# An attention and GLU kernel whose instruction order is planned in Python: other latencies in the planner

## The chip, the cores and the metric

The kernel runs on one core of a Trainium2 chip. The core has a matrix engine (PE, with its weight loads shown apart as PEld), a vector engine (DVE), a scalar engine (ACT), GpSimd (POOL), and a queue for transfers (SP). Each engine takes its instructions in the order in which the program issues them; between engines, semaphores hold an instruction until what it reads is there. The metric is the device time of one execution in microseconds (us); the median of several is given.

## The reference

The input x has 2048 rows of 640 numbers in bf16. There are 32 heads of 20 columns.

```python
x = A_x
h = x + _A_ref(_layernorm(x, axis=-1), A_wqkv, A_wo)
h2 = h + _B_ref(_layernorm(h, axis=-1), B_w_gate, B_w_up, B_w_down)

# _A_ref: q, k, v = heads of x @ wqkv
scores = einsum("bhqd,bhkd->bhqk", q, k) * (20 ** -0.5)
p = softmax(scores, axis=-1)
o = einsum("bhqk,bhkd->bhqd", p, v)        # then o @ wo

# _B_ref: (x @ w_gate) * (x @ w_up), 1728 wide, then @ w_down
```

## The kernel before

**Tiles and stages.** The 2048 queries are cut into five chunks (three of 512, two of 256), the heads into eight groups of four. Scores are made transposed: a tile has 128 keys on the partitions and 512 query columns of one head (or twice 256 for two key tiles). There are 2048 such tiles. Four heads of a group lie on four 32-row strips of PE, so four score matmuls (line 992, mode "R") run side by side. The exponential of a tile is made in one of two ways. ACT takes three tiles at once from the PSUM set SA into a buffer EA, or two from the set SB into a buffer EB (line 1067). DVE takes one tile from one of the banks D0 and D1, with an approximation of four bit-shifted copies: a first pass from PSUM (line 1092), two adds on DVE and one on POOL (lines 1102 and 1100). The buffers are 5 EA, 4 EB and 28 Y. The exponentials are multiplied with V (line 1143, mode "C": four heads on four 32-column strips, adding up in the bank ACC); a tile of ACT needs one such matmul, a tile of DVE four. VX carries a column of ones, so ACC also gets the softmax's sums. When a head group is done, `close_group` copies ACC, sends the sums through DRAM to get reciprocals spread over the partitions, and POOL multiplies.

**Background jobs.** Projections for q, k and v, the output projection and the GLU are jobs of matmuls (line 1316 in strips during attention, line 1293 in whole-array form, mode "D", before and after it). During attention a job takes one of the two D banks; its result is copied out by DVE. Each job has a target, a place in the stream of score tiles by which it should have run.

**The order.** Nothing in the program is ordered by hand. While the kernel is built, Python runs a small event simulation: `now` is the planned time, each engine has a queue of ready instructions (`ready`, `coming`) sorted by a key, and whatever can start at the planned time is issued at once. The costs are formulas (`c_psum(512)` is 0.607 us, `c_fast(512)` 0.208, `c_act(1536)` 1.38, `c_act(1024)` 0.953, a 512-column matmul 0.216), and `LAT`, 0.12 us, lies between the end of any instruction and the start of whatever reads it or uses its buffer again. The planned times are not in the program; what remains is the order on each engine, the choice of which tiles go to DVE, and the choice of buffers.

**What decides around the change.**
- `try_start` takes the ready instruction with the lowest key: DVE's copies of closed groups have -2, evacuations 0, the first pass 1, the adds 2. `finish` tells the readers when they may start.
- `pe_turn` is called when PE is nearly done with what it has (0.03 us before its end, `pe_rest`). It first asks `to_refill`: if a set is free, `refill` issues a score round for it, together with a tile for DVE if a D bank may be had (`d_banks`: one tile on DVE at a time while a background job is ready, else two). If only one set is free, no D bank is, and ACT has more than `THR` = 0.7 us left, the refill waits. Otherwise PE makes up to `ROUNDS` = 4 rounds in columns (`c_round`), each some 0.22 us long, taking exponentials and background matmuls, and stops after the first if `urgent` says that a refill is possible or if a set comes free soon.
- A change between modes R and C costs the planner `SWITCH` = 0.105 us.
- `refill` sets the mark on which ACT's exponential waits, `fill_d` that of DVE's first pass, `emit_piece` the release of the buffer that a matmul of line 1143 has read, `close_group` the mark for ACC's copy, `job_done` the mark for a job's evacuation. Each is the planned end of a matmul plus `LAT`.

Of the kernel before, what the change touches and what calls it, by code (L numbers as in the profile page):

```python
# [14 lines left out]
ACT = mybir.ActivationFunctionType  # L15
# [42 lines left out]


LAT = 0.12  # L60
DMA_LAT = 1.5
SWITCH = 0.105

# [80 lines left out]
def kernel(  # L144
# [89 lines left out]
            heapq.heappush(coming[e], (op.avail, seq[0], op))  # L234
        tick(op.avail)

    def finish(op, t):
        op.done = t
        for u in op.users:
            u.left -= 1  # L240
            u.avail = max(u.avail, t)
            if u.left == 0:
                if isinstance(u, Op):
                    enqueue(u)
                else:
                    release_later(u.avail, u.cb)
        op.users = []
        tick(t)
# [31 lines left out]
    def try_start(e):  # L280
        t = now[0]
        if free[e] > t + 1e-9:
            return False
        c = coming[e]
        while c and c[0][0] <= t + 1e-9:
            _, s_, op = heapq.heappop(c)
            heapq.heappush(ready[e], (op.key, s_, op))
        held = []
        got = None
        while ready[e]:  # L290
            item = heapq.heappop(ready[e])
            op = item[2]
            if op.done is not None:
                continue
            if op.gate is not None and not op.gate():
                held.append(item)
                continue
            other = "POOL" if e == "DVE" else "DVE"
            if op.lock and e in lockt and lockt[other] > t + 1e-9:
                held.append(item)  # L300
                tick(lockt[other])
                continue
            got = op
            break
        for h_ in held:
            heapq.heappush(ready[e], h_)
        if got is None:
            return False
        end = t + (got.dur[e] if isinstance(got.dur, dict) else got.dur)
        free[e] = end  # L310
        if got.lock and e in lockt:
            lockt[e] = end
        if got.hook is not None:
            got.hook(t, end, e)
        got.fn(e)
        finish(got, end + got.lat)
        tick(end)
        return True

# [36 lines left out]
    with tc.manual_schedule():  # L356
# [595 lines left out]
        acs_n = [0]  # L952
        acs_use = [None, None]
        bc_use = [None]
        act_pend = [0]
        dve_units = [0]

        for ci in range(len(CHUNKS)):
# [57 lines left out]
        def refill(name, dbanks):  # L1016

            st = sets[name]
            st["state"] = "full"
            st["free_at"] = 1e9  # L1020
            used = set()
            ditems = []
            for i in dbanks:
                it = take_for_dve(used)
                if it is not None:
                    used.add(it[2])
                    ditems.append((i, it))
            items = []
            for i in range(st["n"]):
                it = take_next(used)  # L1030
                if it is not None:
                    used.add(it[2])
                    items.append(it)
            n = len(items)
            pairs = [(banks[name][i], items[i]) for i in range(n)] + [(banks["D"][i], it) for i, it in ditems]
            ends = rows_into(pairs)
            for q, (i, it) in enumerate(ditems):
                fill_d(i, it, ends[n + q])
            if not n:
                st["state"] = "free"  # L1040
                return
            end = max(ends[:n])
            src = (SA if name == "SA" else SBk)
            eslot = {}

            def hook(t, en, e):
                eslot["i"] = st["efree"].pop(0)
                left = [0]

                def rel():  # L1050
                    left[0] -= 1
                    if left[0] == 0:
                        st["efree"].append(eslot["i"])
                        tick(now[0])
                for i, it in enumerate(items):
                    left[0] += len(it[3])
                for i, it in enumerate(items):
                    queue_pieces(it, 3, [st["e"][eslot["i"]][:, i * 512:(i + 1) * 512]], en + LAT, rel)

                def fr():  # L1060
                    st["state"] = "free"
                    act_pend[0] -= 1
                release_later(en + LAT, fr)
                st["free_at"] = en + LAT

            def fn(e):
                nc.scalar.activation(st["e"][eslot["i"]][:, 0:n * 512], src[:, 0:n * 512], ACT.Exp, scale=SCALE)  # L1067
            z = Mark()
            z.done = end + LAT
            act_pend[0] += 1  # L1070
            add("ACT", c_act(512 * n), fn, (1,), [z], hook=hook, gate=lambda: bool(st["efree"]))

        def fill_d(i, it, end):
            bank = banks["D"][i]
            bank_use["D"][i] = "exp"
            z = Mark()
            z.done = end + LAT
            ys = [None] * 4
            dve_units[0] += 1

            def take(q):
                ys[q] = y_free.pop(0)
                y_owed[0] -= 1

            def hook(t, en, e):
                y_owed[0] += 4
                take(0)

                def fr():
                    bank_use["D"][i] = None  # L1090
                release_later(en + LAT, fr)
            p_ = add("DVE", c_psum(512), lambda e: nc.vector.tensor_scalar(  # L1092
                YT[ys[0]][:, :], bank, scalar1=EXP_A, scalar2=EXP_B, op0=ALU.mult, op1=ALU.add),
                (1,), [z], hook=hook, gate=lambda: len(y_free) - y_owed[0] >= 4)

            def s_op(dst, src_, d, eng, deps):
                def fn(e):
                    o, i_ = YT[ys[dst]][:, :], YT[ys[src_]][:, :]
                    if e == "POOL":
                        nc.gpsimd.tensor_scalar(o, i_, scalar1=float(d), scalar2=1.0, op0=ALU.add, op1=ALU.mult)  # L1100
                    else:
                        nc.vector.tensor_scalar(o, i_, scalar1=float(d), scalar2=None, op0=ALU.add)  # L1102
                return add(eng, {"DVE": c_fast(512), "POOL": c_pool(512)}, fn, (2,), deps, lock=True, lat=LAT,
                           hook=lambda t, en, e: take(dst))
            s1 = s_op(1, 0, SH[1], "DVE", [p_])
            s2 = s_op(2, 0, SH[2], "DVE", [p_])
            s3 = s_op(3, 2, SH[3] - SH[2], "POOL", [s2])
            left = [len(it[3])] * 4
            left[0] += 2
            left[2] += 1  # L1110

            def rel(q):
                left[q] -= 1
                if left[q] == 0:
                    y_free.append(ys[q])
                    tick(now[0])

            for o, q in ((s1, 0), (s2, 0), (s3, 2)):
                after([o], lambda q=q: rel(q))
            for q, o in enumerate((p_, s1, s2, s3)):  # L1120
                after([o], lambda q=q: queue_pieces(it, q, [YT[ys[q]][:, :].bitcast(BF16)], now[0], lambda: rel(q)))
# [11 lines left out]
        def emit_piece(j):  # L1133
# [8 lines left out]
            _, end = pe_issue("C", j, 0.216 * cw / 512)  # L1142
            nc.tensor.matmul(ACC[32 * j:32 * j + 32, 0:cw], lhsT=VX[:, kt, h * VS:h * VS + 32], rhs=ap,  # L1143
                             start=(n == 0), stop=last, tile_position=(0, 32 * j), skip_group_check=True)
            release_later(end + LAT, rel)
            if last:
                acc_state["left"] -= 1
                if acc_state["left"] == 0:
# [8 lines left out]
        def close_group(ci, g, end):  # L1157
            q0, cw = CHUNKS[ci]
            z = Mark()
            z.done = end + LAT  # L1160
            k = ngrp[0] % 2
            d = ngrp[0] % NDS
            ngrp[0] += 1
# [95 lines left out]
        def job_done(jb):  # L1259
            cur_job[0] = None  # L1260
            z = Mark()
            z.done = jb.end + LAT
            op = jb.evac(banks[jb.bank[0]][jb.bank[1]], z)
            bk = jb.bank

# [126 lines left out]
        def pe_turn():  # L1392
# [3 lines left out]
            if spos[0] >= len(stream):  # L1396
                attn["over"] = True
            else:
                r = to_refill()
                if r is not None:  # L1400
                    attn["started"] = True
                    refill(*r)
                    return pe_rest()
            n = 0
            over = attn["over"]
            while n < (1 if over else ROUNDS):
                if n and (urgent() or min(s_["free_at"] for s_ in sets.values()) < pe["end"] - 0.1):
                    break
                c = counts()
                if over and c is not None and sum(c) and c_round(c, False, False):  # L1410
# [7 lines left out]
                if not c_round(c, late and not short(), hold):  # L1418
                    break
                n += 1  # L1420
            return pe_rest() if n else False

        ROUNDS = 4
        WLO, WHI = 20, 50
# [27 lines left out]
        def to_refill():  # L1452
# [3 lines left out]
            if not names:  # L1456
                return None
            db = d_banks()
            if len(names) == 1 and not db and free["ACT"] - now[0] > THR and attn["started"]:
                tick(free["ACT"] - THR)  # L1460
                return None
            return names[0], db

        def urgent():
            return to_refill() is not None
# [73 lines left out]
```

The softmax here doesn't subtract the row's maximum and nothing guards it: scores larger than these inputs give would overflow.

## Time and profile before

| | |
|---|---|
| Median of 13 runs | 871.2 us (863.65 to 874.93) |
| Profiled execution | 873.31 us, of it 871.5 us span, mean granted clock 0.976 |
| PE, busy share of the span | 93% |
| DVE | 85% |
| ACT | 87% |
| POOL | 40% |
| First and last exponential on ACT start | 19.7 and 800.1 us |
| Exponentials on ACT: EA, EB | 319 and 315 |
| Tiles on DVE | 467 |
| Mean granted clock from 250 to 275 us, the lowest stage in attention | 0.84 |

In the lines of groups, "x319" is a count, then come busy time in all and the mean of one in ns, then the idle time of the engine just before these instructions and what ended most of it. In the lines of waits, the numbers are the time in all, the count and the longest. Matmul ends are modelled, so the starts of matmuls are the firm numbers. ACT and DVE instructions that follow each other overlap somewhat in the records: the durations add up to more than the time from start to start.

### The profile page before, as it was taken

The page shows a single profiled execution, that of the slowest core. Times are in us where ns is not written, and L with a number is a line of the kernel's source. Part 1 is how long each engine was busy: PE and PEld are TensorE (multiplying, and loading weights), DVE is VectorE, ACT ScalarE, POOL GpSimd, SP SyncE. Part 2 cuts the span into 40 slices and gives each one's busy share as a digit, 9 for nine tenths or more (in the row PEclk, how much of TensorE's full clock was granted, in tenths as well). Part 3 has the DMA queues.
Part 4 walks back from the last instruction along what each step waited for, and adds up shares of the span by engine and source line. Part 5 has one row for each costly group of instructions (what it writes and reads, how often), then busy time and mean ns, then how long its engine had stood idle before and what let it go on. Part 6 is the DMA issues. An engine that isn't in the chain of part 4 may idle for free.

```text
span 871.5 us, 34285 instructions
## 1 busy us (share of the span) xinstructions
PE 813.9 (93%) x14491; PEld 390.5 (45%) x14491; DVE 736.8 (85%) x2002; ACT 757.4 (87%) x711; POOL 352.4 (40%) x520
## 2 busy tenths in 40 slices
PE   4998999999999999999998999999899999999978
PEld 2432433433323444443233444444355555554856
DVE  6787999888889989998899999988999898896333
ACT  5788999999978999999998999999999999996211
POOL 1033444444443545444455445444545444443000
PEclk9999999999968999999899999999999999999989
DMA  8454221222135301111101002010111111003000
GB/s 271 65 161 127 95 73 39 90 81 75 51 99 129 99 23 46 33 45 31 33 24 32 22 22 53 21 44 27 34 35 41 41 32 35 21 16 52 26 16 16
DMA packets 70537, 49.64 MB, mean 57 GB/s; under 512 B 33712, under 2 KB 66448, under 8 KB 70384
## 3 DMA queue, kind: packets, MB, share of 16 engines
q1 hardware_dynamic: 70384, 47.46, 20.4%
q8 instruction: 113, 1.85, 0.9%
q14 instruction: 40, 0.33, 0.1%
HBM read 30.88 MB, written 10.32 MB: 47 GB/s over the span
## 4 chain that ended last, share of the span: by engine, by line
PE 63%; DVE 18%; ACT 9%; DMA 6%; issue 3%; SPq 0%; POOL 0%; DVEq 0%; ACTq 0%
PE D L1316 21%; PE ACC L1143 17%; PE SA L992 7%; PE D L1293 7%; DVE Y L1092 6%; DVE Y L1102 6%; PE SB L992 5%; ACT EA L1067 5%; PE D L992 5%; ACT EB L1067 4%; DMA dn<-dscr 2%; DMA dscr<-acs 1%; DVE acs L1172 1%; DMA qscr<-HH 1%; DMA R<-in_A_x_dram 1%
## 5 line engine op out<-in xcount | busy, mean ns | idle before, releaser
L1067 ACT ACTIVATE EA<-SA 128x1536 bf16<-128x1536 f32 x319 | 462.3, 1449 | 25.9 <-PE SA L992 17.3
L1100 POOL TENSOR_SCALAR Y<-Y 128x512 uint16<-128x512 uint16 x467 | 304.2, 651 | 415.1 <-DVE Y L1102 270.9
L1092 DVE TENSOR_SCALAR Y<-D 128x512 uint16<-128x512 f32 x467 | 317.9, 683 | 55.5 <-PE SB L992 18.9
L1067 ACT ACTIVATE EB<-SB 128x1024 bf16<-128x1024 f32 x315 | 324.7, 1031 | 19.7 <-PE SB L992 17.1
L1143 PE MATMUL ACC<-Y,VX 128*32 128x512 bf16 (+1 forms) x2356 | 269.0, 344 | 4.9 <-DVE acs L1172 3.5
L1102 DVE TENSOR_SCALAR Y<-Y 128x512 uint16<-128x512 uint16 x934 | 254.4, 318 | 3.1
L1143 PE MATMUL ACC<-EA,VX 128*32 128x512 bf16 (+1 forms) x1186 | 217.7, 346 | 1.2 <-ACT EA L1067 1.1
L992 PE MATMUL D<-QT,KTt 20*128 20x512 bf16 (+1 forms) x589 | 180.1, 343 | 11.7 <-DVE Y L1092 7.6
L992 PEld LDWEIGHTS <-KTt 20*128 20x128 bf16 x2560 | 72.5, 91 | 220.6 <-issue 210.8
L1143 PE MATMUL ACC<-EB,VX 128*32 128x512 bf16 (+1 forms) x785 | 170.8, 346 | 0.3 <-ACT EB L1067 0.3
L1316 PEld LDWEIGHTS <-R 128*32 128x32 bf16 x5370 | 125.0, 96 | 91.0 <-issue 71.4
L1143 PEld LDWEIGHTS <-VX 128*32 128x32 bf16 x4327 | 120.0, 97 | 99.5 <-issue 77.0
L992 PE MATMUL SA<-QT,KTt 20*128 20x512 bf16 (+1 forms) x1186 | 131.6, 345 | 9.3 <-ACT EA L1067 7.8
L1316 PE MATMUL D<-L,R 128*32 128x256 bf16 x3240 | 130.9, 276 | 1.8 <-DVE HH L826 1.4
L992 PE MATMUL SB<-QT,KTt 20*128 20x512 bf16 (+1 forms) x785 | 126.5, 344 | 2.7 <-ACT EB L1067 2.3
L1316 PE MATMUL D<-R 128*32 128x160 bf16 (+1 forms) x2130 | 106.3, 301 | 3.4 <-DVE VX L325 1.1
L826 DVE TENSOR_TENSOR HH<-D,gs 128x256 bf16<-128x256 f32 x112 | 46.8, 418 | 23.2 <-ACT gs L323 22.5
L1201 POOL TENSOR_TENSOR os<-acs,bc 128x512 bf16<-128x512 f32 (+1 forms) x40 | 43.4, 1085 | 48.5 <-DMA bc<-rscr 20.4
L1316 PE MATMUL D<-R,HH 128*32 128x320 bf16 x1136 | 55.3, 301 | 1.9 <-DVE HH L826 1.4
L323 ACT CAST gs<-D 128x256 bf16<-128x256 f32 (+1 forms) x28 | 10.4, 372 | 34.4 <-PE D L1293 34.4
L1316 PEld LDWEIGHTS <-HH 128*32 128x32 bf16 x1136 | 27.1, 96 | 22.5 <-issue 17.5
L325 DVE CAST gs<-D 128x256 bf16<-128x256 f32 x84 | 34.6, 412 | 2.2 <-PE D L1316 1.3
(65 smaller groups left out, 359.3 us busy)
## 6 DMA issues: line engine op xcount, KB each, us to landing
bc<-rscr SPq DMA_DIRECT2D x24, 256.0 KB
KTt<-kscr SPq DMA_DIRECT2D x6, 512.0 KB
QT<-qscr SPq DMA_DIRECT2D x22, 128.0 KB
t<-in_A_x_dram SPq DMA_DIRECT2D x16, 160.0 KB
out_dram<-t SPq DMA_DIRECT2D x16, 160.0 KB
bc<-rscr SPq DMA_DIRECT2D x16, 128.0 KB
R<-in_B_w_gate_dram SPq DMA_DIRECT2D x4, 480.0 KB
R<-in_B_w_up_dram SPq DMA_DIRECT2D x4, 480.0 KB
```

Source lines behind the costliest of these rows:

```text
L323: nc.scalar.copy(o, i)
L325: nc.vector.tensor_copy(o, i)
L826: mu = add("DVE", c_psum(256), lambda e: nc.vector.tensor_tensor(HH[0:M, f, :], bank[0:M, 256:512], GS[k][0:M, :], ALU.mult), EVK, mdeps)
L992: nc.tensor.matmul(bank[:, n * cw:(n + 1) * cw], lhsT=KTt[32 * j:32 * j + Dh, g, kt * P:(kt + 1) * P], rhs=QTt[32 * j:32 * j + Dh, g, 0:cw ...
L1067: nc.scalar.activation(st["e"][eslot["i"]][:, 0:n * 512], src[:, 0:n * 512], ACT.Exp, scale=SCALE)
L1092: p_ = add("DVE", c_psum(512), lambda e: nc.vector.tensor_scalar(YT[ys[0]][:, :], bank, scalar1=EXP_A, scalar2=EXP_B, op0=ALU.mult, op1=AL ...
L1100: nc.gpsimd.tensor_scalar(o, i_, scalar1=float(d), scalar2=1.0, op0=ALU.add, op1=ALU.mult)
L1102: nc.vector.tensor_scalar(o, i_, scalar1=float(d), scalar2=None, op0=ALU.add)
L1143: nc.tensor.matmul(ACC[32 * j:32 * j + 32, 0:cw], lhsT=VX[:, kt, h * VS:h * VS + 32], rhs=ap, start=(n == 0), stop=last, tile_position=(0, ...
L1201: mu = add("POOL", 0.1 + 2.3e-3 * cw, lambda e: nc.gpsimd.tensor_tensor(o[:, 0:cw], a[:, 0:cw], BC[0][:, 0:cw], ALU.mult), (0,), d4 + os_u ...
L1293: nc.tensor.matmul(bank[0:M, c0:c1], lhsT=lhs(0, M), rhs=rhs(), start=first, stop=last, skip_group_check=True)
L1316: nc.tensor.matmul(bank[32 * j:32 * j + 32, c0:c1], lhsT=lhs(32 * j, 32 * j + 32), rhs=rhs(), start=first, stop=last, tile_position=(0, 32 ...
```

## The change

A second latency is introduced, `LATP` = 0.23 us, and used wherever a planned matmul's end releases something: the marks of ACT's exponentials and of DVE's first pass, the release of buffers read by line 1143, the copy of ACC, and the evacuation of a job. All other latencies between engines stay at 0.12. In `finish`, a reader that can run only on the engine that just finished, and is not a transfer, may start at the end itself, without 0.12. The loop of column rounds moves from `pe_turn` into `rounds`; after its first round it now stops when a set will be free up to 0.1 us after PE's planned end, where before it had to be free at least 0.1 us ahead of that end. `act_q` takes the place of the counter `act_pend`, and `dry` and `room_for` are defined and called by nothing. In `to_refill` one condition's parts change places.

```diff
+LATP = 0.23
...
-    def finish(op, t):
+    def finish(op, t, e=None, end=None):
         op.done = t
         for u in op.users:
             u.left -= 1
-            u.avail = max(u.avail, t)
+            u.avail = max(u.avail, end if e is not None and isinstance(u, Op) and u.engs == (e,) and e != "SP" else t)
...
-        finish(got, end + got.lat)
+        finish(got, end + got.lat, e, end)
...
-        act_pend = [0]
+        act_q = {}
...
                 eslot["i"] = st["efree"].pop(0)
+                act_q.pop(name)
...
-                    act_pend[0] -= 1
...
             z = Mark()
-            z.done = end + LAT
-            act_pend[0] += 1
+            z.done = end + LATP
+            act_q[name] = c_act(512 * n)
...
-            z.done = end + LAT
+            z.done = end + LATP
...
-            release_later(end + LAT, rel)
+            release_later(end + LATP, rel)
...
-            z.done = jb.end + LAT
+            z.done = jb.end + LATP
...
+            return pe_rest() if rounds() else False
+
+        ROUND = 0.216
+        SCORE = 0.216 + LATP
+        MARGIN = 0.05
+        AHEAD = 0.1
+
+        def dry():
+
+            return max(free["ACT"], now[0]) + sum(act_q.values())
+
+        def room_for(d):
+
+            t = max(now[0], pe["end"]) + d + (SWITCH if d or pe["mode"] != "R" else 0.0)
+            return t + SCORE + MARGIN <= dry()
+
+        def rounds():
             n = 0
             over = attn["over"]
             while n < (1 if over else ROUNDS):
-                if n and (urgent() or min(s_["free_at"] for s_ in sets.values()) < pe["end"] - 0.1):
+                if n and (urgent() or min(s_["free_at"] for s_ in sets.values()) < pe["end"] + AHEAD):
                     break
...
-            return pe_rest() if n else False
+            return n
...
-            if len(names) == 1 and not db and free["ACT"] - now[0] > THR and attn["started"]:
+            if len(names) == 1 and not db and attn["started"] and free["ACT"] - now[0] > THR:
```

More of the change, by code (lines that the diff above doesn't have):

```diff
@@ L1159, in close_group @@
             z = Mark()
-            z.done = end + LAT
+            z.done = end + LATP
             k = ngrp[0] % 2
```

## The prediction

> **What bounds the kernel now.** I read the page first, then busy time by stage, then the waits, then a timeline inside attention.
>
> ```profile
> PE 813.9 (93%) x14491; PEld 390.5 (45%) x14491; DVE 736.8 (85%) x2002; ACT 757.4 (87%) x711; POOL 352.4 (40%) x520
> L1067 ACT ACTIVATE EA<-SA 128x1536 bf16<-128x1536 f32 x319 | 462.3, 1449 | 25.9 <-PE SA L992 17.3
> L1092 DVE TENSOR_SCALAR Y<-D 128x512 uint16<-128x512 f32 x467 | 317.9, 683 | 55.5 <-PE SB L992 18.9
> L1067 ACT ACTIVATE EB<-SB 128x1024 bf16<-128x1024 f32 x315 | 324.7, 1031 | 19.7 <-PE SB L992 17.1
> L1102 DVE TENSOR_SCALAR Y<-Y 128x512 uint16<-128x512 uint16 x934 | 254.4, 318 | 3.1
> ```
>
> ```profile
> 500.00:600.00 100.00, 97.66 (x1807) 45.13 (x1799) 90.84 (x249) 97.62 (x87) 45.41 (x65) 1.00 0.13 33
> 800.00:872.00 72.00, 63.80 (x517) 49.18 (x515) 25.63 (x63) 12.22 (x34) 2.12 (x4) 0.93 0.12 24
> ```
>
> The stage rows give PE, weight loads, DVE, ACT, POOL, clock. Until 800 us the kernel makes exponentials: 2048 score tiles of 512 columns, 467 by DVE (x467), the rest by ACT in pairs of one EA (3 tiles) and one EB (2). ACT is 97.6% busy there and PE's 97.7% is no work limit: its column rounds hold 396 us of streaming (their columns, four groups side by side, at the 0.21 us for 512 by which rounds follow each other at 345.07 and 345.28 in the timeline) in 543 us of column stretches. So ACT with DVE's share sets 20 to 800 us; the last 70 us are PE with the rest of the GLU.
>
> ```profile
> DVE Y L1092 <- PE SB L992: 18.9, 41, 1.8
> DVE Y L1092 <- PE D L992: 17.8, 33, 1.3
> ACT EA L1067 <- PE SA L992: 17.3, 36, 2.7
> ACT EB L1067 <- PE SB L992: 17.1, 29, 2.2
> PE SA L992 <- ACT EA L1067: 7.8, 20, 0.9
> PE D L992 <- DVE Y L1092: 7.6, 19, 0.8
> ```
>
> What ends ACT's waits is a score round that came late; PE itself waits little.
>
> ```profile
> 341.06 0.38 PE L992 MATMUL D<-QT,KTt 20*128 20x512 bf16 x1
> 341.06 0.39 PE L992 MATMUL SB<-QT,KTt 20*128 20x512 bf16 x2
> ...
> 341.58 1.02 ACT L1067 ACTIVATE EB<-SB 128x1024 bf16<-128x1024 f32 x1
> 341.64 0.68 DVE L1092 TENSOR_SCALAR Y<-D 128x512 uint16<-128x512 f32 x1
> ...
> 342.04 0.39 PE L992 MATMUL SA<-QT,KTt 20*128 20x512 bf16 x3
> ...
> 342.50 1.45 ACT L1067 ACTIVATE EA<-SA 128x1536 bf16<-128x1536 f32 x1
> ...
> 343.83 1.03 ACT L1067 ACTIVATE EB<-SB 128x1024 bf16<-128x1024 f32 x1
> ```
>
> From a score round to its exponential: 0.46 (342.04 to 342.50), 0.52 and 0.58 us. The planner of before reckons 0.216 + 0.12 = 0.336; with 0.23 it is 0.446. ACT starts to ACT start: 0.92 after EB, 1.33 after EA (the planner has 0.953 and 1.38). A pair's floor is thus 2.25; counted over the trace at full clock the pair takes 2.43. The loss over those floors is 55 us, and the records at half clock lose 12 more, which no order gives back.
>
> **The change, part by part.** Nothing is computed otherwise; each edit alters planned times, and through them the order on every engine and which unit goes to DVE. The program carries no times, so only the order counts. `room_for`, `dry`, `SCORE` and `act_q` feed no decision, and the swapped condition in `to_refill` is the same test: nothing, with no cover needed.
>
> *Rounds stop sooner (AHEAD).* A stretch of column rounds ended when a score set would be free 0.1 us before PE's end; PE's next turn is 0.03 before that end. So a set came free up to 0.07 before a turn and still waited for one more round of 0.22: its scores started 0.07 to 0.29 after it was free. With +0.1 it is 0 to 0.22, since PE's turn still makes one round when the set is not yet free: 0.07 us sooner on average. Counted over the trace: a round for SA may start 0.92 - 0.46 = 0.46 us after EB's start without loss. 137 of 307 start at 0.45 to 1.0 and lose 18.7 us; 84 of 304 for SB start at 0.8 to 1.2 (free until 1.33 - 0.46 = 0.87) and lose 10.3. Shifting these by 0.07, capped by each one's loss: 7 + 4 = **-11 us**. Ends: 0 (in-order PE was held by something else) and -29 (all lateness goes). No switch of PE's mode is added: there is still one per score round, 612 of them.
>
> *0.23 from a matmul to DVE: the D bank.* One of two D banks serves DVE while background work holds the other. From a score round to the bank's release the planner had 0.216 + 0.12 + 0.607 + 0.12 = 1.063 us, and will have 1.173. The trace: median 0.495 to DVE's start, 0.683 busy, 0.05 to the next score, 1.23; 151 of 432 intervals between D rounds lie at 1.2 to 1.4, and in 83 the score starts within 0.08 us of DVE's end. Where no D bank is free, the THR rule refills without one as soon as ACT has 0.7 left: SA then has 0.953 - 0.7 = 0.25 us for finding a bank, SB 0.68. So SB rounds carry a D tile 88% of the time, SA rounds 58%. By the planner's sums a tile whose SB round starts 0.6 after EA's start is out of the bank at 0.6 + 1.06 + 0.1 (mode switch) + 0.1 (wait for DVE) = 1.86, which is 0.48 after EB's start at 1.38: the edge of 0.25 and one round of 0.22. 0.11 more is past it. With a chance of 0.9 after an SA round without a tile and 0.4 after one with, the share of SA rounds with a tile is 0.9 / (0.9 + 0.6) = 0.60, near the 58% counted. I estimate that the 0.4 falls to 1 in 7: 0.88 / (0.88 + 0.86) = 51%, and SB to 86: 0.09 tiles a pair fewer, times 316 pairs 28, so 467 becomes about 439. Each tile given to ACT costs 2.43 / 5 = 0.49 us: 28 x 0.49 = **+14 us**. Ends: 0 (the real bank takes 1.23 in either plan) and 65 tiles, +32. What is queued behind a D score on PE is the column rounds; who waits for those is only the release of E and Y buffers.
>
> *0.23 elsewhere.* Planned starts of ACT and evacuations move to where the trace has them, so fewer instructions stand in PE's queue ahead of their buffers: 7.8 + 7.6 + 2.3 (SB) + 5.3 (ACC on acs, EA, Y) = 23 us of PE waits. I take a third, **-8 us**; ends 0 and -23.
>
> *No latency inside one engine.* In the plan DVE idled 0.12 between the first pass and the adds that read it, 467 x 0.12 = 56 us, unless another instruction came in. The trace has 0.60 us from pass to add, as the planner's 0.607 without latency. In it 237 passes are followed by an add, 230 by something else; with the change the add stands first, and an evacuation that would have come into the gap waits 0.2 behind it, with its background bank. For DVE: 55.5 us idle before L1092 is room for 55 tiles at 1.0 us. I take 8 tiles, **-4 us**; ends -12 (24 tiles) and +5 (banks held 0.2 longer in part of the 230).
> The Trainium skill, "VectorE: DVE Perf Modes", section "The DRAIN you can't avoid", speaks against this edit: an instruction issues only when the pipe is empty, and reading what the one before wrote needs a semaphore. By it an estimate would let a dependent add start at or after 0.683, the pass's whole duration, and the edit would be worth 0 or less. The row has 0.60, the same as from the pass to an unrelated copy (0.61), and it decides.
>
> *Queues.* SP keeps its latencies and keys. Each closed group's transfers (sums out and back, reciprocals out, the broadcast, rows into ON) are planned 0.11 later with their copy, and pass nothing of another key. POOL waits 20.4 us for the broadcasts and 271 for DVE's adds, at 40% busy: cover enough for 40 x 0.11 = 4.4 us; without it that would reach the output projections, not the exponentials. The tail: 71 us of PE, same jobs, 0.
>
> Sum: -11 + 14 - 8 - 4 = -9 us. The profiled execution took 873.3 (span 871.5 and 1.8 around it), 2.1 above the median: 864 on its scale, **862** on the median's.
>
> **The rivals.** *Slower: the D bank decides.* ACT's tiles rise. For: a quarter of D rounds start hard on DVE's end. Against: real times in the bank do not change. It decides from 23 / 0.49 = 47 tiles lost; at 65, +32 - 23 = +9: 880.
> *A larger gain.* DVE keeps its 467 since PE's order, not the plan's bank, was late: -11 - 8 - 4 = -23: 848. For: 55.5 us of DVE's idle time ends with score rounds.
> *Nothing.* ACT is at 97.6% and buffers (5 EA, 4 EB, 28 Y) absorb the order: 871.
>
> The Trainium skill, "TensorE: Matmul & The Clock Gate", section "Single matmul latency", has (398 + N) / 2.4 ns, 379 for 512 columns; 0.163 beside 0.216, between 0.12 and 0.23. By it the bank's cycle grows by 0.04, not 0.11, and +14 would be an estimated +5; the rows have 0.46 and more, so I keep 0.23.
>
> **How the numbers follow.** Forecast 0.34 (its own range 855 to 868), larger gain 0.17, nothing 0.11, slower 0.38. A gain or loss counts over 0.3%, 2.6 us, about what runs of this kernel tell apart: faster 0.51, same 0.11, slower 0.38. Range: 848 takes in the larger gain, 884 the slower rival with a little more; I leave 0.2 outside, for both ends of four terms do not come together.
>
> **What would show it.** Tiles on DVE (count of L1092's line) near 439; ACT's idle before its exponentials under 35 us for 45.6; PE's waits for EA and Y under 10 for 15.4; passes followed by an add well above 237. It is wrong if the count drops under 420, if ACT's idle stays, or if attention ends at 800 with a different tail. Stage changes are the largest risk: 23 exponentials whose scores came over 1.0 (SA) or 1.2 us (SB) after the previous start lose 21 us, and a new order can add or drop a few.

## The result: 1.3% slower, and the profile after

The changed kernel takes 881.1 us (median of 11 runs) against 869.6 for the kernel before (48 runs). The ratio is 1.0126, with a 95% interval of 1.0100 to 1.0152: some 11 us more, where 9 us less had been forecast.

The profiled execution took 882.1 us, of it 880.3 span. The last exponential on ACT starts at 810.9 us (800.1 before), and what follows takes 69.4 (71.4 before): the time was lost in attention. These are the groups of the page after; the columns are count, busy time, mean ns, and idle time before with its releaser.

```profile
L1069 ACT ACTIVATE EA<-SA 128x1536 bf16<-128x1536 f32 x320 | 463.9, 1450 | 23.4 <-PE SA L994 18.2
L1094 DVE TENSOR_SCALAR Y<-D 128x512 uint16<-128x512 f32 x456 | 310.8, 684 | 66.0 <-PE SB L994 26.2
L1069 ACT ACTIVATE EB<-SB 128x1024 bf16<-128x1024 f32 x318 | 326.1, 1025 | 24.2 <-PE SB L994 13.1
L1104 DVE TENSOR_SCALAR Y<-Y 128x512 uint16<-128x512 uint16 x912 | 243.2, 312 | 8.4
```

DVE makes 456 tiles instead of 467; ACT's idle time before its exponentials is 47.6 us (45.6 before), so it stayed. What DVE lost shows in part in the last line: 8.4 us of idle time directly before adds, where it was 3.1. The waits on PE's side:

```profile
DVE Y L1094 <- PE SB L994: 26.2, 51, 2.9
ACT EA L1069 <- PE SA L994: 18.2, 27, 2.0
PE SA L994 <- ACT EA L1069: 8.3, 18, 0.9
PE D L994 <- DVE Y L1094: 5.7, 13, 1.1
```

PE's waits for EA and Y are 14.0 us for 15.4: not the fall to under 10 that was forecast.

A timeline of DVE in the changed kernel (start, duration, line, what; one sequence out of the GLU's time) shows where DVE's time goes:

```profile
344.39 0.69 DVE L1094 TENSOR_SCALAR Y<-D 128x512 uint16<-128x512 f32 x1
345.12 0.86 DVE L1104 TENSOR_SCALAR Y<-Y 128x512 uint16<-128x512 uint16 x2
345.94 0.69 DVE L1094 TENSOR_SCALAR Y<-D 128x512 uint16<-128x512 f32 x1
346.55 0.41 DVE L327 CAST gs<-D 128x256 bf16<-128x256 f32 x1
346.99 0.42 DVE L828 TENSOR_TENSOR HH<-D,gs 128x256 bf16<-128x256 f32 x1
```

A pass is followed by a copy that does not read it after 0.61 us (345.94 to 346.55), but by its own add only after 0.73 (344.39 to 345.12); the copy of a gate is followed by its product after 0.44. Counted over the trace: 149 passes are directly followed by their own add, with a median of 0.725 us from start to start, 119 by adds of another tile, with 0.60, and 188 by other things than adds, with 0.61. By the semaphores in the trace, each of the 149 adds waits for the one that DVE's passes raise. A gate copy followed by its product takes 0.448 (82 of 84 times). In the kernel before the same pairs had the same durations but were rarer: 53 and 21, and the gate copy was followed by something else after 0.331 in 63 cases. A reader that stands directly behind its source on DVE thus costs 0.12 us. The change put 231 readers there instead of 74: 149 x 0.125 + 82 x 0.116 = 28 us of DVE's time instead of 9.

### The profile page after: what moved, and what is told of

Read it like the earlier page. It is cut to its first block, busy times and chain, and to the rows that moved or that the text cites. A ratio compares the mean times of both kernels' runs of the same rounds, so it can differ in the third digit from the quotient of the medians.

```text
span 880.3 us, 34202 instructions
## 1 busy us (share of the span) xinstructions
PE 820.3 (93%) x14481; PEld 395.6 (45%) x14481; DVE 735.4 (84%) x1970; ACT 766.2 (87%) x714; POOL 341.2 (39%) x509
## 4 chain that ended last, share of the span: by engine, by line
PE 59%; DVE 20%; ACT 9%; DMA 6%; issue 3%; SPq 1%; POOL 1%; DVEq 0%; POOLq 0%; ACTq 0%
PE D L1318 20%; PE ACC L1145 17%; DVE Y L1094 7%; PE SA L994 6%; PE D L1295 5%; DVE Y L1104 5%; PE SB L994 5%; ACT EA L1069 5%; PE D L994 5%; ACT EB L1069 4%; DMA dn<-dscr 2%; PE SB L1295 1%; DVE lst L430 1%; DMA dscr<-acs 1%; DVE HH L828 1%
## 5 line engine op out<-in xcount | busy, mean ns | idle before, releaser
L1102 POOL TENSOR_SCALAR Y<-Y 128x512 uint16<-128x512 uint16 x456 | 292.8, 642 | 427.8 <-DVE Y L1104 271.4
L1094 DVE TENSOR_SCALAR Y<-D 128x512 uint16<-128x512 f32 x456 | 310.8, 684 | 66.0 <-PE SB L994 26.2
L1145 PE MATMUL ACC<-Y,VX 128*32 128x512 bf16 (+1 forms) x2308 | 273.2, 353 | 5.3 <-DVE acs L1174 5.1
L1104 DVE TENSOR_SCALAR Y<-Y 128x512 uint16<-128x512 uint16 x912 | 243.2, 312 | 8.4
L1145 PE MATMUL ACC<-EB,VX 128*32 128x512 bf16 (+1 forms) x791 | 177.1, 354 | 0.0
L1318 PEld LDWEIGHTS <-R 128*32 128x32 bf16 x5370 | 129.1, 96 | 94.2 <-issue 76.4
L1145 PEld LDWEIGHTS <-VX 128*32 128x32 bf16 x4291 | 123.8, 99 | 99.6 <-issue 78.1
L1318 PE MATMUL D<-L,R 128*32 128x256 bf16 x3240 | 136.1, 276 | 4.2 <-DVE HH L828 3.2
L1318 PE MATMUL D<-R,HH 128*32 128x320 bf16 x1176 | 62.7, 305 | 2.0 <-DVE HH L828 1.3
L1295 PEld LDWEIGHTS <-R 128*128 128x128 bf16 (+1 forms) x300 | 30.7, 105 | 5.7 <-DVE L L327 0.8
```

The source lines that it names most:

```text
L1295: nc.tensor.matmul(bank[0:M, c0:c1], lhsT=lhs(0, M), rhs=rhs(), start=first, stop=last, skip_group_check=True)
L1318: nc.tensor.matmul(bank[32 * j:32 * j + 32, c0:c1], lhsT=lhs(32 * j, 32 * j + 32), rhs=rhs(), start=first, stop=last, tile_position=(0, 32 ...
```

## The experiments

Three theories stood against each other: S (DVE stalls on its own results), D (fewer tiles on DVE, since the plan's bank comes free later) and N (any new order is as much off). Each ratio is to runs of the kernel before that were made beside the experiment's own.

### Each edit alone, and a change without meaning

```diff
 e1: all five marks  -end + LAT   +end + LATP   (LATP = 0.23)
 e2: finish() with the end itself for readers on the same engine
 e3: -pe["end"] - 0.1   +pe["end"] + 0.1
 e4: -LAT = 0.12        +LAT = 0.121
```

> The kernel before with only the matmul latency of 0.23 us in the plan. Its order gives DVE 445 passes for 467 and leaves the adds where they were (111 passes directly followed by an add that reads them, 21 of 84 gate copies directly followed by their product). Theory D (the D bank, fewer tiles for DVE decides): 22 tiles x 0.49 = 11 us more, ACT and DVE waits give back some 5: ratio 1.005 to 1.013. Theory S (DVE stalls on its own results decide): 58 more stalls of 0.115 us, 7 us of DVE, 875 or less: at most 1.006. Theory N (any new order is as much off): as the orders with a planner constant changed by 1%.

> The kernel before with only the edit that lets a reader on the same engine start at the end in the plan. DVE has 460 passes; 151 are directly followed by an add that reads them (53 before), 76 of 84 gate copies by their product (21). Theory S: 98 + 55 = 153 more stalls of 0.115 us, 17.6 us of DVE in a stage where DVE has 55 us of idle time; 7 tiles go to ACT (3.4 us): ratio 1.004 to 1.012, and the pass to its own add takes 0.715 us against 0.60 to anything else. Theory D: 467 to 460 alone, 1.004 at most. The prediction's step had this edit at 0.995.

> The kernel before with only the earlier end of the column rounds. 470 passes on DVE, 78 stalled adds, 24 stalled products. The prediction's step: 11 us less, ratio 0.985 to 0.995, score rounds 0.07 us sooner after a set comes free. Theory S: 28 more stalls, 3 us: 1.000 to 1.004. Theory N: within the spread of the orders with a planner constant changed by 1%.

> The kernel before with 0.121 for 0.12 us as the planner's latency, a change without meaning that gives another order: 465 passes on DVE, 89 stalled adds (53), 22 stalled products (21). Theory N: this alone moves the time by up to 1%, mostly up, since the order of before is a lucky one of many. Theory S: 37 stalls of 0.115, 4 us of DVE: 1.000 to 1.004. Theory D: 1.000 to 1.002.

Measured: e1 1.0048 (1.0011 to 1.0084); e2 1.0030 (0.9985 to 1.0075); e3 1.0003 (0.9967 to 1.0038); e4 1.0074 (1.0035 to 1.0113). The change without meaning moved the time more than any single edit. So one edit's ratio against the kernel before says little: a ratio mixes the edit with the luck of one order. Theory N holds as far as that goes. What the profiles tell is firmer than the times. The groups of e1:

```profile
L1068 ACT ACTIVATE EA<-SA 128x1536 bf16<-128x1536 f32 x323 | 467.4, 1447 | 22.3 <-PE SA L993 15.8 <-PE SB L993 2.6 <-PE D L993 1.1
L1093 DVE TENSOR_SCALAR Y<-D 128x512 uint16<-128x512 f32 x445 | 303.5, 685 | 70.8 <-PE SA L993 25.1 <-PE SB L993 22.5 <-PE D L993 18.2
```

With 0.23 from matmuls alone DVE has 22 tiles fewer, as the bank's sum had said, and idles 70.8 us for 55.5. The groups of e3, with the earlier end of the column rounds alone:

```profile
L1067 ACT ACTIVATE EA<-SA 128x1536 bf16<-128x1536 f32 x318 | 461.0, 1450 | 34.8 <-PE SA L992 27.2 <-PE SB L992 4.5 <-PE D L992 0.5
L1067 ACT ACTIVATE EB<-SB 128x1024 bf16<-128x1024 f32 x314 | 323.0, 1029 | 12.7 <-PE SB L992 9.9 <-PE D L992 1.0
L1092 DVE TENSOR_SCALAR Y<-D 128x512 uint16<-128x512 f32 x470 | 321.1, 685 | 49.7 <-PE SB L992 15.9 <-PE SA L992 13.9 <-PE D L992 9.7
```

ACT idles 47.5 us before its exponentials, as before (45.6): EB's waits fell, EA's rose. Counted over the trace at full clock, a score round for SA starts 0.381 us after the exponential that frees the set has ended (median; 0.376 before), one for SB 0.562 (0.628). SB's rounds came sooner by what had been reckoned; SA's, which were to give 7 of the 11 us, did not.

### Each edit taken out of the changed kernel

```diff
 e5: -finish(got, end + got.lat, e, end)   +finish(got, end + got.lat)
 e6: -LATP = 0.23                          +LATP = 0.12
 e7: -AHEAD = 0.1                          +AHEAD = -0.1
 e8, on the kernel before: -SWITCH = 0.105 +SWITCH = 0.106
```

> The changed kernel without the edit for readers on the same engine (0.23 from matmuls and the earlier end of column rounds stay). 451 passes on DVE, 124 stalled adds (149 with the edit), 25 stalled products (82). Theory S (DVE stalls on its own results): 82 fewer stalls of 0.115, 9 us of DVE, so 0.4 to 0.9% faster than the changed kernel: ratio to before 1.003 to 1.009. Theory D (fewer tiles on DVE): still 16 tiles fewer than before, 1.008 to 1.013.

> The changed kernel with 0.12 for 0.23 us from matmuls (the other two edits stay). 463 passes on DVE, 127 stalled adds, 78 stalled products. Theory D: 4 tiles fewer than before only, 1.000 to 1.004. Theory S: 74 + 57 = 131 more stalls than before, 15 us of DVE: 1.004 to 1.012.

> The changed kernel with the old end of column rounds (the other two edits stay). 445 passes on DVE, 167 stalled adds, 78 stalled products. If the earlier end is worth what was predicted, this is 11 us slower than the changed kernel: 1.020 to 1.028 against before. If it is worth nothing: 1.012 to 1.018.

> The kernel before with 0.106 for 0.105 us as the planner's cost of a change of PE's mode, a change without meaning that gives another order: 460 passes on DVE, 83 stalled adds, 23 stalled products. Theory N: up to 1% from the order alone. Theory D: 7 tiles, 3.4 us, 1.002 to 1.004. Theory S: 32 stalls, 1.000 to 1.004.

Measured: e5 1.0035 (1.0002 to 1.0068); e6 1.0109 (1.0050 to 1.0169); e7 1.0183 (1.0141 to 1.0225); e8 0.9984 (0.9951 to 1.0017). With e1 to e3 and the two kernels all eight combinations are there, and each edit can be read in four pairs, in points of a per cent:

| edit | alone | with one other | with the third | with both | mean |
|---|---|---|---|---|---|
| same engine without latency | +0.30 | +1.06 (AHEAD) | +1.35 (0.23) | +0.91 | +0.9 |
| 0.23 from matmuls | +0.48 | +0.32 (AHEAD) | +1.53 (same engine) | +0.17 | +0.6 |
| AHEAD | +0.03 | -0.13 (0.23) | +0.79 (same engine) | -0.57 | 0.0 |

The edit for readers on the same engine costs in all four pairs; e6, with only 4 tiles fewer but 131 more stalls, is 1.1% slower, against theory D. For 0.23 from matmuls the sign is the same in all pairs too. But with orders that scatter like e4 and e8, four pairs settle the size of neither. AHEAD does nothing on the mean.

### The same order without the waits

An order can be kept, instruction for instruction, while the waits alone go. The adds and products read a constant tile:

```diff
-  o, i_ = YT[ys[dst]][:, :], YT[ys[src_]][:, :]
+  o, i_ = YT[ys[dst]][:, :], YT[ys[src_]][:, :] if e == "POOL" else ONE2
...
-  HH[0:M, f, :], bank[0:M, 256:512], GS[k][0:M, :], ALU.mult)
+  HH[0:M, f, :], bank[0:M, 256:512],
+  GS[k][0:M, :] if attn["over"] else ONE[0:M, 0:256].bitcast(BF16), ALU.mult)
```

> The changed kernel in its own order, instruction for instruction, but the adds on DVE read a constant tile instead of the pass's result, and the GLU's products during attention read it instead of the gate copy: so the later copies of the exponential and the gate's part of the product are left out of what is computed. No add or product can wait for the instruction ahead of it on DVE any more. Theory S: 149 + 82 = 231 stalls of 0.115 us go, 26.6 us of DVE; in the order of before the same takes away 74 stalls, 8.5 us. So the changed kernel gains 0.8 to 1.5% by it (ratio to before 0.998 to 1.005) and before only 0.1 to 0.6%, and most of the difference between the two kernels goes. Theory D (11 tiles fewer on DVE, later banks): it stays 1.008 to 1.013 of before.

> The kernel before in its own order with the same two operands replaced by the constant tile (the later copies of the exponential and the gate's part of the product are left out of what is computed). Theory S: 53 + 21 = 74 stalls of 0.115 us go, 8.5 us of DVE: 0.994 to 0.999. Theory D or N: 0.998 to 1.002, as e9 does not differ from the changed kernel either.

Measured: e9 1.0042 (1.0008 to 1.0075), e10 1.0014 (0.9991 to 1.0036). The same stretch of DVE's timeline as above, in e9:

```profile
344.15 0.69 DVE L1098 TENSOR_SCALAR Y<-D 128x512 uint16<-128x512 f32 x1
344.76 0.86 DVE L1108 TENSOR_SCALAR Y<-one 128x512 uint16<-128x512 uint16 x2
345.70 0.69 DVE L1098 TENSOR_SCALAR Y<-D 128x512 uint16<-128x512 f32 x1
346.31 0.41 DVE L329 CAST gs<-D 128x256 bf16<-128x256 f32 x1
346.64 0.41 DVE L831 TENSOR_TENSOR HH<-D,one 128x256 bf16<-128x256 f32 x1
```

Pass to add 0.61 instead of 0.73, copy to product 0.33 instead of 0.44. DVE's time turns into waiting for score rounds:

```profile
L1098 DVE TENSOR_SCALAR Y<-D 128x512 uint16<-128x512 f32 x456 | 311.4, 686 | 79.9 <-PE SB L998 31.9 <-PE SA L998 20.0 <-PE D L998 19.2
L1108 DVE TENSOR_SCALAR Y<-one 128x512 uint16<-128x512 uint16 x912 | 243.9, 313 | 0.0
```

So taking the waits away gives back 1.26 - 0.42 = 0.84 points, 7.3 us, in the order of the changed kernel (by the two intervals, 0.4 to 1.3 points), and nothing in the order of before, where theory S had asked for 0.1 to 0.6 points. At the middle of that interval, two thirds of the slowdown go with these waits. DVE's own sum had been 28 us, so most of what a wait costs DVE it would otherwise have spent waiting for scores.

The two profiles don't tell where the 7.3 us lie. 108 of the 231 waits stand before 490 us, and up to there the exponentials of e9 are only 1.0 us ahead of those of the changed kernel. At 588 us they are 5.2 us ahead, 1.7 of it gained at 511 us, where only the changed kernel has a record at half clock (3.4 us).

### What is left: the clock, and luck

e11 is the kernel before with 0.23 only on the mark of DVE's first pass (`fill_d`), e12 with `LAT` = 0.119.

> The kernel before with 0.23 us in one place only, the mark that DVE's first pass waits for. 444 passes on DVE, as with 0.23 everywhere (445): the loss of tiles comes from this one place. Theory D: 23 tiles x 0.49 = 11 us, and without what ACT's marks gave back: 1.006 to 1.014, not below e1's 1.0048. Theory N: anywhere from 0.998 to 1.008, unrelated to the tiles.

> The kernel before with 0.119 for 0.12 us as the planner's latency, a third change without meaning: 464 passes, 92 stalled adds, 34 stalled products. The other two gave 1.0074 and 0.9984. Theory N: anywhere between 0.997 and 1.009; it adds to the spread against which the single edits are read. Theory S: 52 stalls more than before, 6 us of DVE: 1.001 to 1.004.

e11 gave 1.0126 (1.0089 to 1.0163): the loss of tiles (444) comes from this mark alone, and it is within what theory D asked. But e12 gave 1.0159 (1.0115 to 1.0203) without any meaning and with 464 tiles, so e11's time can't be told from the luck of an order.

Something else is in the order of the changed kernel. Between 409 and 442 us it has no background matmul (the spell lasted from 417 to 443 before); PE's matmuls thin out, and the granted clock drops. By 20 us, the kernel before (columns: PE, weight loads, DVE, ACT, POOL, then clock, DMA share, GB/s; counts in brackets):

```profile
395.00:415.00 20.00, 19.65 (x333) 7.77 (x328) 17.02 (x45) 19.88 (x19) 8.39 (x13) 1.00 0.11 34
415.00:435.00 20.00, 18.90 (x214) 5.72 (x212) 17.56 (x46) 18.04 (x17) 9.21 (x13) 0.83 0.12 34
```

and the changed kernel:

```profile
395.00:415.00 20.00, 18.38 (x317) 7.45 (x315) 16.54 (x45) 19.93 (x19) 8.96 (x14) 1.00 0.11 34
415.00:435.00 20.00, 18.97 (x134) 4.15 (x133) 14.83 (x39) 14.35 (x13) 8.01 (x13) 0.51 0.09 25
```

For 20 us the clock is at half, and ACT does 14.35 us of work where it did 18.04. The 20 us stretch is in both profiles of this order (the changed kernel and e9); the order of before has 6.8 us there in one profile and nothing in the other (e10). The Trainium skill, "TensorE: Matmul & The Clock Gate", section "What's actually happening", has a gate that halves PE's clock after an idle window of about 3.4 us. The records here agree with the window's length: the drops last whole multiples of 3.41 us, here 3.4, 6.8, 13.7 or 20.5 us. They don't show it idle: in the 6.8 us ahead of the drop at 415 us PE's longest pause is 0.95 us (4.2 ahead of the drop at 74 us), so PE was sparse here rather than idle. To see what it costs, score matmuls were issued twice wherever no background job was ready:

```diff
+ dry_spell = attn["started"] and not bg_wanted()
...
+ if dry_spell:
+     nc.tensor.matmul(...)   # the same score matmul, the same bank
  nc.tensor.matmul(bank[:, n * cw:(n + 1) * cw],
```

> The changed kernel in its own order, but wherever no background job is ready, each score matmul is issued twice into the same bank (359 of 2560): useless work that keeps PE busier, 0.22 us more per score round there. Theory C (the sparse PE loses its clock and with it time): the half-clock time in attention, 60 us in both profiles of this order, falls under 25, the stretch at 416 us goes, and the time falls by 4 to 10 us against the changed kernel: ratio to before 1.001 to 1.008. If the clock has another cause: the extra matmuls delay some 90 score rounds by 0.22 us, up to 5 us more: 1.013 to 1.018.

> The kernel before in its own order with the same doubled score matmuls where no background job is ready (385 of 2560). Theory C: half-clock time in attention 34 us in the profile of before falls under 20: 0.990 to 0.998, which would beat both kernels. If the clock has another cause: 1.000 to 1.006.

Measured: e13 1.0240 (1.0188 to 1.0292), e14 1.0067 (1.0038 to 1.0096). e13 by stages:

```profile
415.00:435.00 20.00, 18.36 (x220) 5.89 (x219) 18.18 (x46) 17.81 (x17) 9.93 (x15) 1.00 0.08 23
615.00:655.00 40.00, 39.49 (x532) 19.09 (x526) 22.15 (x60) 23.74 (x20) 13.95 (x20) 0.50 0.07 18
```

In time, e13 met neither range and e14 lies just above the second. The stretch at 415 us is gone (220 matmuls, clock 1.00, ACT 17.81), as theory C asked. But a longer one appeared at 615 us, in the other spell without background matmuls (604 to 647 us): 40 us at half clock, with PE busy for 39.49 of them and ACT for 23.74. There 532 matmuls in 40 us did not bring the clock back, where 220 in 20 us had held it. That the sparse PE lowers the clock at 415 us is therefore likely, and no rule follows from it. In e14 the half-clock time within attention fell from 34 to 17 us (27 in e10, the same order), and the kernel still got slower: the doubled matmuls seem to cost more than the clock gave. What the stretch at 415 us costs the changed kernel remains an estimate, (18.04 - 14.35) / 20 of it, about 4 us. It is near the 0.42 points that e9 left over, as are the 11 tiles (5 us); these two weren't separated, and why the stretch went to 615 in e13 stays open.

The clock may be worth more than that. In the 103 runs of the kernel before that the ratios of e1 to e18 rest on, all of one order, the mean granted clock lies between 0.972 and 0.994, and the time falls by 5.2 us for each 0.01 of it (correlation -0.84). The runs of the changed kernel have 0.966 on the mean, those of before 0.984. If that slope held from one order to another, which no run shows, the lower clock would go with 9 of the 11 us. It is not another name for the waits: e9 has 0.969, so by the slope only 1.6 of its 7.3 us would be clock. Waits, clock and tiles then come to more than the 11 us that were lost; what the new order gains elsewhere, or how far the three overlap, these runs don't tell.

The last runs ask whether the changed planner is worse or its order unlucky: e15 is the changed kernel with `LAT` = 0.121, e16 the kernel before with `SWITCH` = 0.104, and e17 and e18 are e15 and e12 with the constant tile of e9.

> The changed kernel with 0.121 for 0.12 us as the planner's latency between other engines, a change without meaning: 450 passes on DVE, 161 stalled adds, 79 stalled products. Theory S (with the plan's zero latency inside DVE every order has some 230 stalls): 1.010 to 1.020, as the changed kernel. Theory N (its order is unlucky by chance): it falls near the nulls of before, 1.000 to 1.010.

> The kernel before with 0.104 for 0.105 us as the cost of a change of PE's mode: 467 passes, 82 stalled adds, 27 stalled products. A fourth null; the others gave 1.0074, 0.9984 and 1.0159. Theory N: 0.997 to 1.012. Theory S: 35 stalls, 4 us of DVE: 1.000 to 1.004.

> The order of the changed kernel with 0.121 (1.0176 of before), with adds and products on DVE reading the constant tile (the later copies of the exponential and the gate's part of the product are left out of what is computed). 161 + 79 = 240 stalls go. Theory S: as in the changed kernel, 0.6 to 1.2% less: 1.006 to 1.012. Otherwise 1.015 to 1.020.

> The order of the kernel before with 0.119 (1.0159 of before), with the same two operands replaced by the constant tile (the same parts are left out). 92 + 34 = 126 stalls go, half as many as in the changed kernel. Theory S for the spread of orders: 0.4 to 0.8% less, 1.008 to 1.012. If this order is slow for another cause (its score rounds, its clock): 1.013 to 1.018.

| order | self-reads on DVE | ratio | same order, without the waits |
|---|---|---|---|
| before | 53 + 21 | 1 | 1.0014 (0.9991 to 1.0036) |
| before, 0.106 (e8) | 83 + 23 | 0.9984 | |
| before, 0.104 (e16) | 82 + 27 | 0.9991 (0.9959 to 1.0023) | |
| before, 0.121 (e4) | 89 + 22 | 1.0074 | |
| before, 0.119 (e12) | 92 + 34 | 1.0159 | 1.0083 (1.0048 to 1.0118) |
| changed | 149 + 82 | 1.0126 | 1.0042 (1.0008 to 1.0075) |
| changed, 0.121 (e15) | 161 + 79 | 1.0176 (1.0124 to 1.0229) | 1.0107 (1.0060 to 1.0154) |

The five orders of the old planner average 1.0042, the two of the new one 1.0151, but they overlap: e12 is slower than the changed kernel. Over all the orders above, the five with the edit for the same engine (e2, e6, e7, e15 and the changed kernel) average 1.0125, the nine without it 1.0047, with a scatter of 0.6 points inside each group. So one order can hide or feign what the edit costs. Taking the waits away gives back 0.84 points in the changed kernel (0.4 to 1.3), 0.76 in e12 (0.2 to 1.3) and 0.69 in e15 (0.0 to 1.4, not clear of zero), and nothing in before. They are not a count times a price: 126 of them cost e12 about as much as 231 cost the changed kernel. And e12 and e15 keep 0.8 to 1.1 points without them, whose cause these runs don't show. For e12 it is hardly the clock: its runs have 0.980, by the slope above 2 to 3 of its 14 us.

## Why the prediction was wrong

**No latency inside one engine (-4 us): this step failed.** The prediction took "0.60 us from pass to add" from the trace. The 237 pairs behind it are of two kinds, which the group view and the names do not keep apart. In 184 of them, the adds were those of an earlier tile; 53 passes were followed by their own. The times from start to start would have told them apart: none lies between 0.61 and 0.68 us. The kernel before has them too, for instance here:

```profile
343.40 0.69 DVE L1092 TENSOR_SCALAR Y<-D 128x512 uint16<-128x512 f32 x1 [0.17 <-PE SB L992]
344.13 0.40 DVE L1102 TENSOR_SCALAR Y<-Y 128x512 uint16<-128x512 uint16 x1
```

0.73 us. So 0.607 + 0.12 was right, and the gap that the planner left behind a pass was no waste: it is the time that DVE needs for its own result, and in which another instruction could start. Planned at zero, the add goes first and the stall is paid. Where 4 us of gain had been forecast, the edit cost 0.9 points on the mean of its four pairs, a figure that the scatter of orders leaves uncertain, and the stalls 7.3 us (3.6 to 11) in the order itself. The step also dismissed the sentence of the Trainium skill that reading what the instruction before wrote needs a semaphore ("VectorE: DVE Perf Modes", "The DRAIN you can't avoid"). The rows agree with it: the add waits, and starts 0.725 us after a pass of 0.684. The same section says not only that the next instruction can't start before the pipe is empty, but also that one which is not held starts earlier. The prediction left that out, and the rows show it: an unrelated instruction starts at 0.60. The mark "passes followed by an add well above 237" came true (268) and meant a loss.

**Rounds stop sooner (-11 us): nothing.** The sum rested on score rounds 0.07 us sooner. SB's did come sooner, by 0.07, 0.12, 0.02 and 0.07 us (medians) in the four pairs with and without AHEAD. SA's, which were to give 7 of the 11 us, did not: 0.381 us for 0.376 in e3. For SA, the reckoning of the break rule in planned times didn't carry over into when PE really reached the score round, and the pairs' times moved by 0.0 points on the mean.

**The D bank (+14 us): the count came near, by another way.** 0.23 on that one mark takes DVE from 467 to 444 tiles (e11), with the other marks to 445 (e1); 439 had been reckoned. But the sum took the tiles from SA's rounds (58% with a tile to 51%) and left SB's nearly alone (88% to 86%). Counted over the traces, in which some matmul records are missing, SA rounds that carry a tile are 181 before, 183 in e1 and 184 in e11; SB rounds are 268, 243 and 240. The whole loss fell on SB, so the near count was luck. Unforeseen was also that AHEAD gives tiles back: 470 for 467, 451 for 445, 456 for 445. So 11 tiles were lost instead of 28. The price of a tile was not confirmed, as orders scatter by more.

**0.23 elsewhere (-8 us): not shown.** PE's waits for its readers stayed (14.0 for 15.4 us for EA and Y). ACT's small losses (under 0.8 us each, at full clock, over the floors of 0.92 and 1.33) fell by 3.8, 3.9, 4.8 and 9.5 us in the four pairs with and without 0.23, 5.5 on the mean: less than the 11 us that 22 tiles were reckoned to cost. But by the same kind of count they fall by 6.7 us in e11, where DVE's mark alone has 0.23. So this fall can't be put down to the other marks.

**The rival that came nearest** was the slower one, at 880 for 881, but by another mechanism: it asked for 65 tiles lost, and 11 were.

**The clock was put at nothing.** The prediction counted 12 us lost at half clock, "which no order gives back", and took them as the same after the change. But the order moves them: in attention the profile of the changed kernel has 61 us at half clock (58 in e9) where before had 34 (27 in e10). By the slope above that goes with up to 9 us, an estimate and not shown apart from the rest.

**What no step had** is the scatter of the orders: a planner's constant changed by 1% or less moves the time by -0.2 to +1.6%, and the kernel before lies at the fast end of that. The prediction called anything over 0.3% a gain or loss; that holds for repeating one order, and not for judging an edit of the planner by one order.

## What to carry to other kernels

Before putting a latency between two instructions of one engine at zero, look for pairs where the second really reads the first, by the names of the buffers and not by lines: here 0.725 us for a reader and 0.60 for a stranger. When a greedy planner orders the work, first run a few changes without meaning and see how far they scatter; an edit is only judged against that, or in a fixed order with the one wait taken away. And a mark that is more truthful can still cost: 0.23 on one mark took 23 tiles from DVE. That the threshold of 0.7 us, set against the old mark, is the reason was argued and not tested.

## What the runs showed of the hardware

On DVE, the time from an instruction to the next one depends on whether the next reads its result and waits for it: an instruction of 0.684 us is followed by an unrelated one after 0.60, by a reader after 0.725; one of 0.414 after 0.331 and 0.448. PE's granted clock fell to half in stretches of 3.4 to 41 us not only where PE was idle but where its matmuls thinned to 134 in 20 us (from 317), and in the stretch from 415 us more matmuls (220 in 20 us), even useless ones, went with a clock of 1.00. From 615 us, 532 in 40 us went with half clock, so a count of matmuls alone doesn't tell the clock. Within one order, 0.01 less mean clock went with 5.2 us more (103 runs).
